# A Fourier-mixing and low-rank MLP kernel: w1's load, the filter copies, V's reorder and stage 3 of the first batch rearranged

## The chip, the cores and the metric

The kernel runs on one core of one Trainium2 chip. Such a core has five engines that run side by side: TensorE (PE in the profile; PEld is its weight load), VectorE (DVE), ScalarE (ACT), GpSimd (POOL) and SyncE (SP). Each works off its own list of instructions in order, and they wait for one another by semaphores. Transfers between the device's memory and SBUF, the on-chip memory, are made by 16 DMA engines; a transfer is issued by an instruction on the queue of SyncE or GpSimd, and the issuing queue is in order too. Matmul results go to PSUM banks, from which VectorE or ScalarE copy them.

The metric is the device time of one execution, in microseconds (us).

## The reference: what is computed

`x` has 8 batches of 3136 rows and 256 columns. Each is filtered along its rows in the frequency domain; the result `u0` is mixed along the rows through a matrix of rank 32, added to itself, and sent through a two-layer MLP with a residual:

```python
X = np.fft.rfft(x, axis=1)
Y = X * (filt_r + 1j * filt_i)[None, :, :]
u0 = np.fft.irfft(Y, n=3136, axis=1)
h = u0.transpose(0, 2, 1) @ U @ V            # U 3136x32, V 32x3136
u = u0 + h.transpose(0, 2, 1)
out = u + np.maximum(u @ w_ch1, 0.0) @ w_ch2  # 256x1024, 1024x256
```

All inputs and the output are float32.

## The kernel before

The transform of length 3136 is split as 49 x 64, and every part of it is a matmul with a constant matrix in float16. Per batch there are four stages.

- Stage 1 (`f1`, for batches 0 and 1 `f1_turned`): 49-point transforms of x, which comes in four chunks `x(b, c)` (`load_x`, 392 KB each, cast to float16 on the way, on GpSimd's queue). It leaves frequencies k1 = 0 to 24. For batches 0 and 1 the result is turned by TensorE (`turn`, L297); later ones go through device memory (`ct1`).
- Stage 2 (`mid`, L366): 64-point transforms, in pairs of k1: (1,2), (3,4), a single (0), (5,6) and so on to (23,24). DVE multiplies each result `pz` by the filters `fab` into `uv` (L374). `fab` holds the filters for 25 values of k1 in 64 partitions, copied once into the other 64 (`spread_filters`): k1 0 to 4 by DVE, 5 to 12 by DVE and ACT, 13 to 24 by GpSimd in two copies, one per filter (L164).
- Stage 3 (`s3`, inside `mid`, L330): the inverse 64-point transform of a pair into a bank `pe`, two matmuls in batch 0, which ACT copies to `e3` (L340). In batch 0 it runs two pairs behind stage 2. The rows then go to `eb`, arranged otherwise: mostly by a write to device memory for two pairs at a time (`ct2`, L348) and a load back (`load_e2(b, part, hs)`, L398, by part and by half of `eb`), both on SyncE's queue. In batch 0 the last two pairs, (21,22) and (23,24), go by eight single-row DMAs straight to `eb`, half of them on GpSimd's queue and half on SyncE's (L344).
- Stage 4 (`s4`, L438): `eb` (97 rows: 32 of the rank-32 part, 65 of frequencies) times `sv` into `ut`, 16 banks of eight matmuls. `sv`'s first 32 rows are V, reordered from `vnat` by one GpSimd copy (`v_rows`, L200).

The rank-32 part: U's transform is made first (`u_hat`), turned by TensorE into `uh` (`u_turned`: one ACT copy `tp`, 25 + 4 transposes, three ACT copies, L222 to L233). `rank` multiplies `e3` by `uh` (L405; in batch 0 first 20 products, then, after the last pairs, the rest), ends in `h1`, and DVE spreads `h1` over 64 places of `eb` in four copies (L420).

The MLP works on 49 groups of 512 rows, each in eight steps. A step is one `mm1` (L470, with w1, relu by ACT at L473) of group n and one `mm2` (L493, with w2, plus the residual at L485) of group n - 1. Between the steps a list `plan` deals out the pieces of the next batch's stages. The loop at L564 writes that list down: batch 1's stage 1 is dealt over steps 1 to 7 of group 0, its stage 2 begins at step 8.

So batch 0's transform stands alone at the start, written out by hand (L524 to L558). It is this part that the change touches. The order there: U's transform; stage 1 of batch 0; 13 steps of `mid(0)`, with `u_turned` after the tenth and `load_e2(0, 0)` after the eleventh; `load_e2(0, 1, [0])`; the first 20 rank products; the last two pairs of stage 3 with three more row loads; the rest of `rank`; four pieces of batch 1's stage 1, mixed with 13 matmuls into a bank `pw` that nothing reads; then stage 4.

GpSimd's queue holds, in order: U, the eight DMAs of x(0, 0 to 3), the filters in twelve DMAs, three memsets and V, `sv`'s constants, x(1, 0), the two filter copies, V's reorder, four single-row DMAs, and then a tiny copy out of `eb` into `seen`, whose only use is that it waits for row loads, w1's load, a second such copy, x(1, 1 to 3), and w2:

```python
nc.gpsimd.tensor_copy(seen[64:66], eb[64:66, 8, 0:4])
nc.gpsimd.dma_start(w1sb, moe_w_ch1.rearrange("(h dd) c -> dd h c", h=2))
nc.gpsimd.tensor_copy(seen[64:96], eb[64:96, 40, 0:4])
for c in range(1, 4):
    load_x(1, c)
nc.gpsimd.dma_start(w2sb, moe_w_ch2.rearrange("(t cc) e -> cc t e", t=8))
```


Of the kernel before, what the change touches and what calls it, by code (L numbers as in the profile page):

```python
# [10 lines left out]
F16 = mybir.dt.float16  # L11
# [5 lines left out]
NQ, NR = 49, 64  # L17
NK = 25
DM = 256
RANK = 32  # L20
# [59 lines left out]
def kernel(  # L80
# [11 lines left out]
    nc = tc.nc  # L92
# [66 lines left out]
    def spread_filters(i):  # L159
        s = slice(PARTS[i], PARTS[i + 1])  # L160
        copies = ((nc.vector.tensor_copy, nc.vector.tensor_copy), (nc.vector.tensor_copy, nc.scalar.copy),
                  (nc.gpsimd.tensor_copy, nc.gpsimd.tensor_copy))[i]
        for f, copy in enumerate(copies):
            copy(fab[64:128, f, s, :], fab[0:64, f, s, :])  # L164

    for i in range(3):
        load_filters(i)
# [3 lines left out]
    for t in a20:  # L171
        nc.gpsimd.memset(t[64:128], 0)

# [19 lines left out]


    uh = cst.tile([128, NK + 4, RANK], F16)
    seen = cst.tile([128, 4], F16)
    nc.gpsimd.memset(uh[64:128, 0, :], 0)

    def v_rows():
        nc.gpsimd.tensor_copy(sv[0:RANK], vnat.rearrange("p (q r) -> p r q", r=NR))  # L200
# [18 lines left out]

    def u_turned():  # L220
        tp = sb.tile([RANK, 4, 128], F16, tag="tp", bufs=1, name="tp")
        nc.scalar.copy(view(tp, 0, [[64, 8], [32, 2], [8, 4], [1, 8]]), view(tu, 128 * 20, [[64, 8], [8, 2], [16, 4], [1, 8]]))  # L222
# [84 lines left out]
    def mid(b, tag="z"):  # L307
# [14 lines left out]
        def s3(ks, uv, o):  # L322
# [5 lines left out]
            ms = (gmp, gsmp) if direct or not ks[0] else (gm, gsm)  # L328
            for f, w in enumerate(ms if b == 0 else ms[:1]):
                nc.tensor.matmul(pe[:, 0:n], w, uv[:, f, o:o + n], start=(f == 0), stop=(b > 0 or f == 1))  # L330
# [52 lines left out]
        for it in todo:  # L383
            s3(*it)
            if b:
                yield
# [143 lines left out]
    v_rows()  # L530
    for i in range(13):
        next(mids[0])
        if i == 9:
            u_turned()
        if i == 10:
            load_e2(0, 0)
    load_e2(0, 1, [0])
    next(ranks[0])
    next(mids[0])
    next(ranks[0])  # L540
# [10 lines left out]
    nc.gpsimd.tensor_copy(seen[64:66], eb[64:66, 8, 0:4])  # L551
    nc.gpsimd.dma_start(w1sb, moe_w_ch1.rearrange("(h dd) c -> dd h c", h=2))
    nc.gpsimd.tensor_copy(seen[64:96], eb[64:96, 40, 0:4])
    for c in range(1, 4):
        load_x(1, c)
# [63 lines left out]
```

## Time and profile before

| | |
|---|---|
| median of 3 runs | 519.34 us (519.16 to 520.23) |
| profiled execution | 519.37 us, span of the profile 517.6 us |
| TensorE busy | 493.0 us, 95% of the span |
| ScalarE, VectorE, GpSimd busy | 376.7, 351.1 and 85.1 us |
| first stage-4 product (L438) | at 43.72 us |
| first mm1 (L470) | at 49.27 us |
| first mm2 (L493) | at 58.98 us |

How to read the profile. A line of a timeline gives the start in us from the start of the span, the length, the engine, the line of the kernel, the operation, what it writes and reads, and in brackets how long the engine idled before it and what ended that. A line of the waits gives an engine and line, what it waited for, and the time in total, the number of waits and the longest. A line of the chain gives start, length and what was under way; the chain is followed back from the last instruction, at each step to what released it. A line of the stretches gives busy time and instructions of each engine, then the granted clock of TensorE, the share of the DMA engines in use and what they moved. "DMA x<-in_x_dram" is a transfer from its issue to its landing.

### The profile page before, as it was taken

The page shows a single profiled execution, that of the slowest core. Times are in us where ns is not written, and L with a number is a line of the kernel's source. Part 1 is how long each engine was busy: PE and PEld are TensorE (multiplying, and loading weights), DVE is VectorE, ACT ScalarE, POOL GpSimd, SP SyncE. Part 2 cuts the span into 40 slices and gives each one's busy share as a digit, 9 for nine tenths or more (in the row PEclk, how much of TensorE's full clock was granted, in tenths as well). Part 3 has the DMA queues.
Part 4 walks back from the last instruction along what each step waited for, and adds up shares of the span by engine and source line. Part 5 has one row for each costly group of instructions (what it writes and reads, how often), then busy time and mean ns, then how long its engine had stood idle before and what let it go on. Part 6 is the DMA issues. An engine that isn't in the chain of part 4 may idle for free.

```text
span 517.6 us, 11940 instructions
## 1 busy us (share of the span) xinstructions
PE 493.0 (95%) x4839; PEld 352.6 (68%) x4839; DVE 351.1 (68%) x469; ACT 376.7 (73%) x705; POOL 85.1 (16%) x119
## 2 busy tenths in 40 slices
PE   4687899999999999999999999999999999999997
PEld 4345566776777777777767777777777766776665
DVE  5866699489847976688747975689756995631112
ACT  6675779867986689667986689667985777666662
POOL 6775010011001120012010120011010010101110
PEclk9989999999999999999999999999999999999999
DMA  8967936848776487928776497819885146212213
GB/s 194 182 187 167 178 87 189 251 167 190 204 228 246 86 197 214 289 82 191 203 240 234 90 209 225 303 49 205 222 249 185 62 144 202 86 42 84 81 42 123
DMA packets 67287, 88.09 MB, mean 170 GB/s; under 512 B 4875, under 2 KB 51787, under 8 KB 67232
## 3 DMA queue, kind: packets, MB, share of 16 engines
q0 software_dynamic: 14768, 41.65, 32.5%
q1 hardware_dynamic: 52464, 45.68, 29.2%
q8 instruction: 38, 0.62, 0.5%
q14 instruction: 17, 0.14, 0.1%
HBM read 55.07 MB, written 47.64 MB: 198 GB/s over the span
## 4 chain that ended last, share of the span: by engine, by line
PE 86%; DMA 6%; DVE 3%; POOL 2%; issue 1%; ACT 0%; SPq 0%; POOLq 0%
PE pc L493 32%; PE phh L470 32%; PE pu L438 4%; PE pc L485 4%; PE pf L245 4%; PE pe L330 4%; DMA x<-in_x_dram 4%; PE pz L366 4%; DVE uv L374 2%; PE ph L405 1%; DMA fab<-in_filt_r_dram 1%; POOL fab L164 1%; POOL x L127 1%; DMA eb<-ct 1%; DVE uv L378 0%
## 5 line engine op out<-in xcount | busy, mean ns | idle before, releaser
L473 ACT ACTIVATE h<-phh 128x512 f16<-128x512 f32 x392 | 235.9, 603 | 88.0 <-PE phh L470 86.6
L470 PE MATMUL phh<-ut,w1sb 128*128 128x512 f16 (+7 forms) x896 | 233.3, 352 | 1.2 <-DMA w1sb<-in_moe_w_ch_dram 1.2
L493 PE MATMUL pc<-w2sb,h 128*128 128x256 f16 x1568 | 234.1, 272 | 0.0
L493 PEld LDWEIGHTS <-h 128*128 128x128 f16 x1568 | 151.6, 97 | 90.4 <-issue 0.2
L500 DVE COPY och<-pc 128x512 f32<-128x512 f32 x98 | 67.6, 690 | 99.6 <-PE pc L485 98.4
L374 DVE TENSOR_TENSOR uv<-pz,fab 128x1024 f16<-128x1024 f32 (+1 forms) x104 | 120.9, 1179 | 13.7 <-PE pz L366 11.1
L505 POOL DMA_DIRECT2D out_dram<-och x48 | 39.1, 815 | 403.3 <-DVE och L500 395.7
L470 PEld LDWEIGHTS <-w1sb 128*128 128x128 f16 x896 | 77.4, 97 | 20.0 <-DMA w1sb<-in_moe_w_ch_dram 1.3
L340 ACT CAST e<-pe 128x512 f16<-128x512 f32 x96 | 56.5, 591 | 20.2 <-PE pe L330 19.6
L445 DVE CAST ut<-pu 128x392 f16<-128x392 f32 x92 | 48.5, 558 | 17.8 <-PE pu L438 17.8
L250 ACT CAST asb<-pf 98x512 f16<-98x512 f32 x96 | 57.3, 599 | 0.2
L485 PE MATMUL pc<-idn,ut 128*128 128x128 f16 (+1 forms) x400 | 54.0, 219 | 0.0
L420 DVE COPY eb<-h 32x4096 f16<-32x4096 f16 x32 | 38.2, 1233 | 16.2 <-ACT h L417 16.1
L330 PE MATMUL pe<-uv,m 128*128 128x512 f16 (+1 forms) x117 | 42.1, 380 | 3.1 <-DVE uv L374 2.1
L485 PEld LDWEIGHTS <-ut 128*128 128x128 f16 (+1 forms) x400 | 38.1, 98 | 5.2 <-issue 0.8
L438 PE MATMUL pu<-sv,eb 97*128 97x49 f16 x1024 | 39.1, 185 | 0.9 <-DMA eb<-e 0.9
L366 PE MATMUL pz<-a,m 128*128 128x512 f16 x96 | 36.6, 383 | 2.2 <-DVE a L299 1.6
L438 PEld LDWEIGHTS <-eb 97*128 97x128 f16 x1024 | 36.3, 96 | 2.0 <-issue 1.2
L245 PE MATMUL pf<-x,ws 98*98 98x256 f16 x192 | 36.6, 273 | 0.0
L378 DVE TENSOR_TENSOR uv<-uv 64x1024 f16<-64x1024 f16 (+1 forms) x49 | 30.9, 630 | 1.7
L379 DVE TENSOR_TENSOR uv<-uv 64x1024 f16<-64x1024 f16 (+1 forms) x49 | 30.7, 627 | 0.7
L245 PEld LDWEIGHTS <-ws 98*98 98x98 f16 x192 | 22.4, 125 | 9.1 <-issue 0.4
(78 smaller groups left out, 221.5 us busy)
## 6 DMA issues: line engine op xcount, KB each, us to landing
out_dram<-och POOLq DMA_DIRECT2D x48, 512.0 KB, 4.0
ct<-e SPq DMA_DIRECT2D x47, 256.0 KB
eb<-ct SPq DMA_DIRECT2D x46, 256.0 KB
x<-in_x_dram POOLq DMA_DIRECT2D x28, 392.0 KB, 7.8
ct<-asb SPq DMA_DIRECT2D x24, 384.0 KB
a<-ct SPq DMA_DIRECT2D x18, 512.0 KB
x<-in_x_dram POOLq DMA_DIRECT2D x4, 384.0 KB, 8.0
ws<-ws SPq DMA_DIRECT2D x1, 600.2 KB
```

The source lines that it names most:

```text
L245: nc.tensor.matmul(pf[0:98, 256 * s:256 * s + 256], ws[:, (8 * c + j) * 98:(8 * c + j + 1) * 98], t[:, j, :], start=(s == 0), stop=True, s ...
L250: nc.scalar.copy(dst, src)
L330: nc.tensor.matmul(pe[:, 0:n], w, uv[:, f, o:o + n], start=(f == 0), stop=(b > 0 or f == 1))
L340: nc.scalar.copy(t[:, 2 * (i % 2):2 * (i % 2) + 2, :].rearrange("p k d -> p (k d)"), pe)
L366: nc.tensor.matmul(pz, a2m, src[:, k:k + 2, :].rearrange("p k d -> p (k d)"), start=True, stop=True)
L374: nc.vector.tensor_mul(uv[:, :, o:o + n], zin, fin)
L438: nc.tensor.matmul(pu[:, NQ * i:NQ * i + NQ], eb[:, 8 * n + i, d], sv[:, 8 * g + i, :], start=(i == 0), stop=True, skip_group_check=True)
L470: nc.tensor.matmul(ph[:, o:o + n], w1sb[:, dh, 128 * t:128 * t + 128], utv(b)[:, dh, t0:t0 + n], start=(dh == 0), stop=(dh == 1), skip_gro ...
L473: nc.scalar.activation(h, ph, RELU)
L485: nc.tensor.matmul(d, w, idn, start=False, stop=(dh == 1), skip_group_check=True)
L493: nc.tensor.matmul(o, gr.h[tt][:, 128 * i:128 * i + 128], w2sb[:, tt, :], start=(tt == 0), stop=False, skip_group_check=True)
L500: nc.vector.tensor_copy(gr.och[:, i - 1:i + 1, :], gr.pc.rearrange("p (j d) -> p j d", d=DM))
```

## The change

It has seven parts, all in the work for batch 0 ahead of the first group.

1. The memsets of `a20` and `uh` go ahead of the filter loads on GpSimd's queue.
2. GpSimd's two filter copies become four: both filters for k1 13 to 18, then both for 19 to 24.
3. w1's load goes on GpSimd's queue behind these copies and ahead of V's reorder. In its old place, between the two `seen` copies, stands x(1, 1).
4. V's reorder is split by r: GpSimd does 0 to 31; DVE does 32 to 63, behind its last product of stage 2.
5. `u_turned` runs after the ninth step of `mid(0)` instead of the tenth, and its copy `tp` after the eighth. `load_e2(0, 0)` follows the ninth step instead of the eleventh.
6. Stage 3 of (21,22) goes ahead of the first 20 rank products; (23,24) stays behind them.
7. Ahead of stage 3's matmuls for the eight pairs from (9,10) on stands one 128x512 matmul into the same bank, which the next one overwrites. The 13 matmuls into `pw` become seven.

```diff
         copies = ((nc.vector.tensor_copy, nc.vector.tensor_copy), (nc.vector.tensor_copy, nc.scalar.copy),
                   (nc.gpsimd.tensor_copy, nc.gpsimd.tensor_copy))[i]
-        for f, copy in enumerate(copies):
-            copy(fab[64:128, f, s, :], fab[0:64, f, s, :])
-
-    for i in range(3):
-        load_filters(i)
+
+        for s in (slice(PARTS[2], 19), slice(19, NK)) if i == 2 else (s,):
+            for f, copy in enumerate(copies):
+                copy(fab[64:128, f, s, :], fab[0:64, f, s, :])
...
     for t in a20:
         nc.gpsimd.memset(t[64:128], 0)
+
+    uh = cst.tile([128, NK + 4, RANK], F16)
+    nc.gpsimd.memset(uh[64:128, 0, :], 0)
+
+    for i in range(3):
+        load_filters(i)
...
-    def v_rows():
-        nc.gpsimd.tensor_copy(sv[0:RANK], vnat.rearrange("p (q r) -> p r q", r=NR))
+
+    def v_rows(copy, a, z):
+        copy(sv[0:RANK, a:z], vnat.rearrange("p (q r) -> p r q", r=NR)[:, a:z])
...
+    tp = cst.tile([RANK, 4, 128], F16)
+
+    def u_ordered():
+        nc.scalar.copy(view(tp, 0, [[64, 8], [32, 2], [8, 4], [1, 8]]), view(tu, 128 * 20, [[64, 8], [8, 2], [16, 4], [1, 8]]))
+
     def u_turned():
-        tp = sb.tile([RANK, 4, 128], F16, tag="tp", bufs=1, name="tp")
-        nc.scalar.copy(view(tp, 0, [[64, 8], [32, 2], [8, 4], [1, 8]]), view(tu, 128 * 20, [[64, 8], [8, 2], [16, 4], [1, 8]]))
...
             ms = (gmp, gsmp) if direct or not ks[0] else (gm, gsm)
+            if b == 0 and ks[0] > 8:
+
+                nc.tensor.matmul(pe, m64[:, 0:128], m64[:, 0:512], start=True, stop=True, skip_group_check=True)
             for f, w in enumerate(ms if b == 0 else ms[:1]):
...
-        for it in todo:
+        for n, it in enumerate(todo):
             s3(*it)
-            if b:
+            if b or n == 0:
                 yield
...
     spread_filters(2)
-    v_rows()
+    nc.gpsimd.dma_start(w1sb, moe_w_ch1.rearrange("(h dd) c -> dd h c", h=2))
+    v_rows(nc.gpsimd.tensor_copy, 0, 32)
     for i in range(13):
         next(mids[0])
-        if i == 9:
+        if i == 7:
+            u_ordered()
+        if i == 8:
+            load_e2(0, 0)
             u_turned()
-        if i == 10:
-            load_e2(0, 0)
     load_e2(0, 1, [0])
+    next(mids[0])
     next(ranks[0])
     next(mids[0])
+    v_rows(nc.vector.tensor_copy, 32, NR)
     next(ranks[0])
...
-    for i in range(13):
+    for i in range(7):
         if i < 4:
             next(f1s[1])
-        nc.tensor.matmul(pw, m64[:, 0:128], m64[:, 0:512], start=(i == 0), stop=(i == 12))
+        nc.tensor.matmul(pw, m64[:, 0:128], m64[:, 0:512], start=(i == 0), stop=(i == 6))
 
     nc.gpsimd.tensor_copy(seen[64:66], eb[64:66, 8, 0:4])
-    nc.gpsimd.dma_start(w1sb, moe_w_ch1.rearrange("(h dd) c -> dd h c", h=2))
+    load_x(1, 1)
     nc.gpsimd.tensor_copy(seen[64:96], eb[64:96, 40, 0:4])
-    for c in range(1, 4):
+    for c in range(2, 4):
         load_x(1, c)
```

More of the change, by code (lines that the diff above doesn't have):

```diff
@@ L192 @@
             nc.vector.memset(rows.bitcast(mybir.dt.uint32), 0)
-    uh = cst.tile([128, NK + 4, RANK], F16)
     seen = cst.tile([128, 4], F16)
-    nc.gpsimd.memset(uh[64:128, 0, :], 0)
-    def v_rows():
-        nc.gpsimd.tensor_copy(sv[0:RANK], vnat.rearrange("p (q r) -> p r q", r=NR))
+    def v_rows(copy, a, z):
+        copy(sv[0:RANK, a:z], vnat.rearrange("p (q r) -> p r q", r=NR)[:, a:z])
     tu = eb[0:RANK, 0:12, :].rearrange("p r d -> p (r d)")
```

## Prediction, made before the changed kernel was run

> **What bounds the kernel now.** I read the page first, then the stretches of the span, then the waits and the chain of the first 80 us, then GpSimd's and the DMA queue's timelines there. Page, parts 1 and 2:
>
> ```profile
> span 517.6 us, 11940 instructions
> PE 493.0 (95%) x4839; PEld 352.6 (68%) x4839; DVE 351.1 (68%) x469; ACT 376.7 (73%) x705; POOL 85.1 (16%) x119
> PEclk9989999999999999999999999999999999999999
> ```
>
> TensorE is busy nearly throughout; one slice, from 25.9 us on, has a lower clock. The stretches (columns: engine busy, granted clock, DMA share, GB/s):
>
> ```profile
> 32.00:36.00 4.00, 4.00 (x29) 1.54 (x29) 3.76 (x4) 2.47 (x6) 2.43 (x1) 0.60 0.37 87
> 44.00:49.00 5.00, 4.03 (x139) 3.91 (x135) 4.37 (x9) 3.89 (x8) 3.27 (x6) 1.00 0.86 145
> 49.00:59.00 10.00, 6.71 (x67) 3.83 (x68) 3.61 (x11) 7.06 (x20) 1.08 (x2) 1.00 1.08 186
> 59.00:79.00 20.00, 18.92 (x161) 13.02 (x160) 18.39 (x25) 13.90 (x25) 1.33 (x2) 1.00 0.54 119
> 79.00:500.00 421.00, 421.00 (x4077) 303.30 (x4075) 288.92 (x375) 316.05 (x583) 47.65 (x65) 1.00 0.60 174
> ```
>
> From 79 us TensorE has no gap, and from 59 to 79 it lacks 1.1 us. The change touches only work before that, so what it does to the start of the first mm2 (58.98 us) goes into the end unchanged: a later piece cannot start sooner than TensorE comes to it, nor does TensorE wait there. The stretch 49 to 59 lacks 3.3 us of TensorE, with the DMA engines full. Its waits and those ahead of it:
>
> ```profile
> PE pf L273 <- DMA x<-in_x_dram: 4.1, 5, 1.6
> PE phh L470 <- DMA w1sb<-in_moe_w_ch_dram: 1.2, 1, 1.2
> DVE uv L374 <- POOL fab L164: 1.2, 1, 1.2
> PE pu L438 <- DMA eb<-e: 0.9, 1, 0.9
> ```
>
> Of the 4.1 us for x, 3.0 lie after 49 us (1.62, 0.38 and 1.02, ending at 51.92, 54.08 and 56.86, just after x(1,1), x(1,2) and x(1,3) land). The other three name w1, the copies of the filters, and the rows of `eb` that stage 4 reads. The chain before them:
>
> ```profile
> 26.01 2.75 POOL fab L164
> ...
> 29.93 1.23 DVE uv L374
> ...
> 40.17 0.78 SPq L398
> ...
> 41.00 2.97 DMA eb<-ct
> ...
> 46.04 10.78 DMA x<-in_x_dram
> ```
>
> So: filter copy, stage 3, row loads issued by SyncE, then the x loads, which GpSimd's queue lets go only after the rows and behind w1:
>
> ```profile
> 28.81 5.62 POOL L200 COPY sv<-vnat 32x3136 f16<-32x3136 f16 x1
> 37.92 3.04 POOL L344 DMA_DIRECT2D eb<-e  x4 [3.49 <-ACT e L340]
> 41.72 0.31 POOL L551 COPY seen<-eb 2x4 f16<-2x4 f16 x1 [0.77 <-DMA eb<-ct]
> 42.22 1.04 POOL L552 DMA_DIRECT2D w1sb<-in_moe_w_ch_dram  x1 [0.20 <-issue]
> 44.92 1.66 POOL L127 DMA_DIRECT2D x<-in_x_dram  x3 [0.30 <-PE pu L438]
> ```
>
> The sum is made against the profiled execution, 519.37 us (span 517.6 and 1.8 around it), 0.03 above the median of 519.34.
>
> **Part by part.**
>
> *Early memsets.* Two of 0.31 and one of 0.15 us move ahead of the filter loads, where GpSimd idles 1.67 us for the landing of an x load. Cost nothing; were that wait gone, the filters would be 0.77 late. V, `sv` and x(1,0) are issued some 0.6 sooner: no one waits for them.
>
> *Filter copies in four.* A 64x3072 copy takes 2.74, so a 64x1536 one about 1.4 (between 1.37 and, with a small copy's 0.18 added, 1.55). The first starts at 23.32 as now, the second waits for the imaginary filter (landed 25.13) and ends near 26.7, the last near 29.5 instead of 28.8. DVE's product for (13,14) no longer waits 1.22 for them. Late next is its matmul: pz starts at 27.46 and lands 0.4 later, so the product starts at 27.85 instead of 28.79: 0.94 sooner. Products for (19,20) and up need the second pieces, at 31.9, after 29.5.
>
> *u_turned one step sooner, its ACT copy ahead.* 25 transposes (0.75) now stand before pz for (17,18), and the four of `pd` wait for `tp`, which ACT reaches at 29.5 (behind the two 0.9 turns and one e copy): TensorE passes them at 30.3, so that product starts at 30.7 instead of 31.06. Of the 0.94 some 0.35 is left; but the 0.21 that DVE now waits at 32.48 goes, so the last product ends near 35.35 instead of 35.97: 0.6 sooner (0 to 1.2).
>
> *Eight unread products.* Each 128x512 matmul has a pitch of 0.215, 1.7 in all. DVE's pitch per pair is 1.13; pz, unread product and two pe matmuls take 0.86, so they run while TensorE waits for DVE. At half clock the cover is gone: 1.72 per pair for 1.13, some 1.2 us in a stretch of 3.41; that is the other end. They fill the time ahead of the stretch that now has half clock, 32.79 to 36.20, in which pe matmuls stand 0.43 apart and the 20 rank products take 1.06; the 24 of a later batch take 0.77 in the chain, so some 0.65. I take the full clock, since TensorE's gaps of 0.94 and 0.36 ahead of it (at 30.07 and 31.86) are what the products and the moved transposes fill.
>
> *Last pairs sooner.* Pair (21,22) goes ahead of the rank products: pe at 34.25, its e copy done at 35.5 (now 37.63). Pair (23,24) follows them: rank products 34.7 to 35.35, the unread one, pe landing at 36.2, e copy done at 36.8 (now 38.12). h1 and DVE's copies into `eb` follow at 38.35 instead of 39.63. GpSimd and SyncE each issue four single-row DMAs (0.53 to 0.60 apiece); two now go at 35.5, two at 36.8.
>
> *load_e2(0, 0) two steps sooner.* On SyncE's queue it goes behind the write of (11,12) and waits for that of (7,8), which lands at 31.09; nothing behind it is due before 32.8. load_e2(0,1,[0]) then waits for the write of (15,16), issued at 32.85. Such writes landed in 2.3 (now, DMA engines idle) to 4.7 (first one, engines full). At 2.3 it issues at 35.1 and stops nothing; with w1 and the row loads moving beside it I take 36.0, worst 37.5. Queued behind it are four single rows and load_e2(0,2,[0]): 0.5 plus 4 x 0.58 bring that to 38.85 (38.0 by the e copy alone; 40.3 at worst; now 40.17). The first stage-4 product came 3.55 after that issue, so it comes at 42.3 instead of 43.72: **1.4 sooner**, bounds 2.1 sooner and 0.1 later. GpSimd's last row is issued near 38.2 and lands 3.7 later, at 41.9.
>
> *V's reorder shared.* GpSimd's half is 2.8 (30.6 to 33.4, free until 35.8). DVE's half has 1568 elements; at the product's 1.13 per 1024 it takes 1.7, at GpSimd's rate 2.8, so it runs from 35.35 to 37.1 or 38.2, and DVE's next work is due at 38.35. Nothing, and nothing in its place later: the copies into `eb` wait on h1.
> One thing speaks against putting it on DVE: GpSimd's fourth row DMA, issued at 39.55 while DVE's copy of 39.63 to 40.84 ran, took 1.41 against 0.53 to 0.57 for its neighbours. The Trainium skill ("SBUF — State Buffer", "Who interferes with whom") says that a DVE copy in a two-port mode and GpSimd exclude each other, also while GpSimd writes a DMA's descriptors. The trace agrees in this row (GpSimd done 0.12 after DVE). By that rule, if DVE's half is such a copy, GpSimd's rows wait until 37.2, the last meets the copy at 38.35, and they land near 42.3 instead of 41.9: the sum is unchanged and its best end 0.7 shorter.
>
> *w1 early.* Issued at 29.5 (0.91 as for w2, which shares its size, up to 1.04), it moves 512 KB. In the engine-full stretch x loads of 392 KB land 2.15 apart (51.88, 54.03), so w1 costs 2.8 of DMA time, from 31.5 to 34.5 where the DMA engines are now busy 0.03 to 0.9. It lands long before 47. What it collides with is counted above (36.0 for 35.1).
>
> *x(1,1) in w1's place, fewer fillers.* x(1,1) is issued near 41 after the first `seen` copy and lands near 46 (5 later, as x(1,1) itself took 7.0 with w1 ahead); x(1,2), x(1,3) and w2 follow without w1 ahead. Now w2 lands 7.05 after x(1,1) (58.93 and 51.88), so about 53.2. Six filler matmuls less, 1.3 us, end at 40.1 instead of 42.57: no one waits for them; TensorE idles 2.2 before stage 4 (now 0.9).
> TensorE's way from the first stage-4 product to the first mm2: 4.85 to the last copy of `ut` (43.72 to 48.55; w1 now adds 0.7), then ACT's work: seven relu at 0.49 and six f1 pairs at 0.43, 6.0 after a first 0.6, and 0.45 for mm1: 11.9 in all. Now it is 15.26 (43.72 to 58.98). **3.4 sooner**, if loads come as reckoned; w2 at 53.2 is ahead of the mm2 at 42.3 + 11.9 = 54.2. Bounds: TensorE's own time there (5.7 for 6.0 and 0.6) 4.3 sooner; loads late as in the first rival 1.0 sooner.
>
> Sum: 1.4 + 3.4 = 4.8; 519.4 - 4.8 = **514.6** us, in its own right 513.3 to 515.6 (both best ends together would be 513.0).
>
> **Rivals.**
> 1. *The loads gate again.* If the second `seen` copy passes at 44.45 as now, since x(1,1) moves beside the last rows, x(1,2) starts at 47.5 and w2 lands 8.0 later, 55.5, or 56.5 if its small packets share with x(2,0). Gain 2.5 to 3.5: 516.3. For it: DMA share 1.08 from 49 to 59. Against: the rows are issued 1.3 sooner.
> 2. *w1 takes from the rows what the order gives.* Load_e2(0,2,[0]) issues at 40.2 as now; only 3.4 is gained: 516.0. For it: everything reads and writes through the same 16 engines, at 0.88 to 1.08 from 36 to 39. Against: those engines idle at 32 to 34.
> 3. *The clock halves in stage 4.* TensorE idles from 40.1 to 42.3. In the trace a lower clock follows a thin stretch (29.38 to 32.79, TensorE busy 2.35 of 3.41) and lasts 3.41; at half pace a stage-4 bank takes up to 0.53 instead of 0.26, so 3.41 us do the work of 1.7: 516.3, or 515.5 if evacuation hides half. Against: 49.86 to 53.27, busy only 1.79, was not followed by one. The Trainium skill ("TensorE: Matmul & The Clock Gate", "The HAM clock gate") says that the gate judges free-running windows of 3.4 us; the 3.41 of the trace agrees, and by that rule it hangs on where the window lies.
> 4. *Slower: SyncE stops behind load_e2(0,1,[0]).* The queue is in order; the write of (15,16) shares the engines with w1 and 512 KB of rows. Each us that it lands after 36 delays all rows by one. At 40.8 the gain is gone; slower by 0.2% from 41.9, that is if the write takes 9. At 43.5: 522. Against: the longest seen is 4.7.
> 5. *Hidden anyway:* the stretch from 59 to 79, where DVE has 18.39 of 20, would have to take back what came before: 519.4. Against: its work starts with x(1,1..3) and moves along.
>
> **How the numbers follow.** Forecast 0.58, rival 1 0.13, 2 0.10, 3 0.08, 4 0.07, 5 0.04. From 513.3 over rivals 1 to 3, with rivals 1 and 2 together at 517.4, the range is 513.3 to 517.4 and leaves about 0.15 out, mostly 4 and 5. Faster by over 0.2% 0.89 (0.2%, 1.04 us, is about what runs of this kernel can tell: 519.16 to 520.23), within 0.04, slower 0.07.
>
> **What would show it.** No wait of DVE for GpSimd's `fab`; no half clock before 40 us; last e copy at 36.8, first stage-4 product at 42.3, first mm1 near 47.1 without a wait for w1, first mm2 near 54.2; TensorE's waits for x after 45 us under 0.5 instead of 3.0; from there every row 4.8 sooner. Wrong if w2 lands after 55, SyncE's load_e2(0,1,[0]) issues after 37.5, or a half-clock stretch lies between 42 and 47.

## The result, and the profile after

The changed kernel is slower: 523.35 us (median of 16 runs) against 520.12 us for the kernel before (16 runs on the same chip), a ratio of 1.0054 with an interval of 1.0036 to 1.0072. Forecast were 514.6 us and a range of 513.3 to 517.4. The two profiled executions, 523.45 and 519.37 us, differ by 4.08 us, and this is where that lies:

| us from the span's start | forecast | before | after |
|---|---|---|---|
| last copy of `e3` for stage 3 done | 36.8 | 38.1 | 37.5 |
| write of (15,16) to device memory: issued, landed | 32.85, 36.0 | 33.52, 35.79 | 33.47, 39.87 |
| SyncE issues load_e2(0,2,[0]) | 38.85 | 40.17 | 43.06 |
| first stage-4 product | 42.3 | 43.72 | 46.59 |
| first mm1 | 47.1 | 49.27 | 55.05 |
| first mm2 | 54.2 | 58.98 | 63.05 |

The last row says it all: 63.05 - 58.98 = 4.07 of the 4.08. What lies behind the first mm2 takes as long as before. The stretches of after (engine busy, granted clock, DMA share, GB/s):

```profile
44.00:49.00 5.00, 2.41 (x52) 2.44 (x53) 1.28 (x3) 0.97 (x2) 0.88 (x3) 0.51 0.74 159
49.00:59.00 10.00, 8.69 (x125) 6.69 (x123) 4.34 (x9) 5.38 (x12) 2.71 (x5) 0.56 0.96 159
59.00:79.00 20.00, 19.46 (x179) 13.32 (x176) 16.92 (x28) 15.07 (x34) 2.23 (x4) 1.00 0.41 90
79.00:500.00 421.00, 420.30 (x4068) 302.68 (x4066) 292.20 (x379) 316.35 (x584) 46.87 (x64) 1.00 0.61 175
```

From 79 us TensorE is nearly as full as before (420.30 of 421 us), which carried the sum as the prediction said. What is new is a clock of 0.51 and 0.56 from 44 to 59. Ahead of it stands a long wait. SyncE's timeline before:

```profile
34.06 1.22 SPq L398 DMA_DIRECT2D eb<-ct  x2
36.05 0.36 SPq L348 DMA_DIRECT2D ct<-e  x1
36.52 0.51 SPq L398 DMA_DIRECT2D eb<-ct  x1
37.65 2.42 SPq L344 DMA_DIRECT2D eb<-e  x4
40.17 2.15 SPq L398 DMA_DIRECT2D eb<-ct  x3
```

and after (L406 is before's L398, L356 its L348, L352 its L344):

```profile
31.91 1.22 SPq L406 DMA_DIRECT2D eb<-ct  x2
33.47 2.09 SPq L356 DMA_DIRECT2D ct<-e  x2
39.89 0.52 SPq L406 DMA_DIRECT2D eb<-ct  x1
40.50 2.46 SPq L352 DMA_DIRECT2D eb<-e  x4
43.06 2.15 SPq L406 DMA_DIRECT2D eb<-ct  x3
```

load_e2(0, 0) is issued 2.15 us sooner (31.91), as meant. The line at 33.47 holds the writes of (15,16) and (19,20), the latter at 35.20. Then SyncE stands still for over 4 us: load_e2(0,1,[0]) waits for the write of (15,16), and that lands 6.4 us after its issue, where before it took 2.27. Four single rows whose data are ready at 37.5, and load_e2(0,2,[0]), stand behind it.

Why the write takes so long is to be seen in the DMA queues from 31.5 to 34.5, first of before, then of after (q1 carries SyncE's transfers, q0 GpSimd's; packets, MB, share of the 16 engines):

```profile
q1 hardware_dynamic: 329, 0.16, 18.9%
```

```profile
q0 software_dynamic: 202, 0.41, 91.5%
```

After has no q1 line at all. In these 3 us only w1 moves, although SyncE has issued four transfers by then. In steps of one microsecond the same view gives:

| MB moved in | 31-32 | 32-33 | 33-34 | 34-35 | 35-36 | 36-37 | 37-38 | 38-39 | 39-40 |
|---|---|---|---|---|---|---|---|---|---|
| after: q0 | 0.04 | 0.12 | 0.17 | 0.17 | 0.01 | 0.01 | 0 | 0.05 | 0.07 |
| after: q1 | 0.01 | 0 | 0 | 0.01 | 0.33 | 0.35 | 0.35 | 0.24 | 0.02 |
| before: q1 | 0.26 | 0.01 | 0 | 0.16 | 0.16 | 0.32 | 0.27 | 0.28 | 0.18 |

w1 takes 3.5 us of all 16 engines (its shares from 31 to 37 add up to 3.5). Then everything that SyncE issued from 31.18 to 35.20 (writes of (11,12), (15,16), (19,20), two loads; five times 256 KB, 1.31 MB) drains together, 1.30 MB from 34 to 40, at 0.33 to 0.35 MB per us from 35 to 38, and all but 0.02 MB is through at 39.

That rest still matters. The trace records the end of such a transfer in 16 parts. Of the write of (15,16) fifteen came by 38.68 and the last at 39.87, 1.19 us later (in before 0.01), and from 39.1 to 40.3 q1's packets follow each other about every 0.02 us, as on one engine alone. As the drain begins, at 34.97, there is a transfer of 16 KB that belongs to neither queue and takes 0.96 us of one engine; in the view from 34 to 35:

```profile
q8 instruction: 1, 0.02, 6.0%
```

The last part is 0.9 to 1.5 us late in after, e2_late, only_w1, w1_e2 and fill34, where this transfer starts between 32.7 and 35.6; it is at most 0.21 late in the other kernels of the table below, where the transfer starts by 31.6 or, in before and ow_ahead, meets nearly idle engines. No run tests whether it is the cause.

What TensorE meets. Its timeline and waits in after:

```profile
46.59 0.49 PE L446 MATMUL pu<-sv,eb 97*128 97x49 f16 x8 [5.68 <-DMA eb<-ct]
46.97 0.54 PE L446 MATMUL pu<-sv,eb 97*128 97x49 f16 x8
51.30 0.49 PE L446 MATMUL pu<-sv,eb 97*128 97x49 f16 x8 [1.09 <-DMA eb<-ct]
55.05 1.87 PE L478 MATMUL phh<-ut,w1sb 128*128 128x512 f16 x4 [0.22 <-DVE ut L453]
63.05 0.60 PE L501 MATMUL pc<-w2sb,h 128*128 128x256 f16 x4
```

Two stretches cut at the change of the clock:

```profile
40.69:44.11 3.42, 0.21 (x2) 0.00 (x0) 2.97 (x3) 0.10 (x2) 0.17 (x1) 1.00 0.42 115
44.11:57.76 13.65, 9.86 (x156) 8.28 (x157) 4.68 (x9) 5.29 (x11) 3.30 (x7) 0.50 0.86 157
```

TensorE idles for 5.7 us and then has half clock for 13.65 us, in which the banks of stage 4 come 0.433 apart instead of 0.262. The ninth bank (51.30) also waits 1.09 for the last row loads. The chain shows why they are late (start, length, what):

```profile
43.06 0.78 SPq L406
43.90 0.58 SPq L406
44.52 6.65 DMA eb<-ct
```

and GpSimd's timeline what moves beside them:

```profile
44.17 0.58 POOL L127 DMA_DIRECT2D x<-in_x_dram  x1
48.81 0.18 POOL L565 COPY seen<-eb 32x4 f16<-32x4 f16 x1 [4.05 <-DMA eb<-ct]
```

x(1,1), in w1's old place, is issued 0.35 before the last row load, which takes 6.65 us (3.40 in before). One trace below, w1_back's, comes from a slow execution (533.46 us, clock 0.95), so only its transfers are compared, and the ratios leave out that run and one of 1049 us of fill34.

### The profile page after: what moved, and what is told of

It reads as the page before. It is cut to its first block, busy times and chain, and to the rows that moved or that the text cites. A ratio compares the mean times of both kernels' runs of the same rounds, so it can differ in the third digit from the quotient of the medians.

```text
span 521.7 us, 11949 instructions
## 1 busy us (share of the span) xinstructions
PE 497.5 (95%) x4841; PEld 357.0 (68%) x4841; DVE 352.8 (68%) x470; ACT 376.2 (72%) x705; POOL 81.7 (16%) x121
## 4 chain that ended last, share of the span: by engine, by line
PE 85%; DVE 3%; DMA 1%; ACT 1%; SPq 1%; issue 0%
PE pc L501 32%; PE phh L478 32%; PE pu L446 5%; PE pc L493 4%; PE pf L250 4%; PE pe L338 3%; PE pz L374 3%; DVE uv L382 2%; DMA eb<-ct 1%; PE ph L413 1%; ACT h L481 0%; DVE uv L386 0%; DVE uv L387 0%; DVE och L508 0%; SPq L352 0%; DVE a L304 0%
## 5 line engine op out<-in xcount | busy, mean ns | idle before, releaser
L382 DVE TENSOR_TENSOR uv<-pz,fab 128x1024 f16<-128x1024 f32 (+1 forms) x104 | 120.9, 1179 | 13.4 <-PE pz L374 11.9
L513 POOL DMA_DIRECT2D out_dram<-och x48 | 39.1, 814 | 402.7 <-DVE och L508 395.1
L348 ACT CAST e<-pe 128x512 f16<-128x512 f32 x96 | 56.7, 591 | 19.3 <-PE pe L338 18.4
L446 PE MATMUL pu<-sv,eb 97*128 97x49 f16 x1024 | 41.9, 189 | 6.8 <-DMA eb<-ct 6.8
L446 PEld LDWEIGHTS <-eb 97*128 97x128 f16 x1024 | 38.9, 99 | 8.0 <-issue 7.2
```

The source lines that it names most:

```text
L348: nc.scalar.copy(t[:, 2 * (i % 2):2 * (i % 2) + 2, :].rearrange("p k d -> p (k d)"), pe)
L382: nc.vector.tensor_mul(uv[:, :, o:o + n], zin, fin)
L446: nc.tensor.matmul(pu[:, NQ * i:NQ * i + NQ], eb[:, 8 * n + i, d], sv[:, 8 * g + i, :], start=(i == 0), stop=True, skip_group_check=True)
```

## Experiments

Each kernel was run against the kernel before, with its own runs of it beside it; the ratio is to that. To set an experiment against the changed kernel, compare its ratio with 1.0054. The profiled executions differ by a us or two where half clock strikes early (a stretch at 16 to 18 us moves all later times), so the distances between events say more than single times. In these kernels all is computed as in the kernel before; only matmuls whose result nothing reads are more or fewer. The recorded expectations weigh these theories: R, the row path (SyncE behind the write) delays all; C, the half clock itself is the loss; S, the rows' own transfers are slow, wherever w1 stands; later P, only w1 and load_e2(0, 0) together make the write late; and Q, it depends on when w1's packets come relative to the writes.

| kernel | write of (15,16): issued, landed | first stage-4 product | first mm1 | first mm2 | half clock from (length) | ratio, interval |
|---|---|---|---|---|---|---|
| before | 33.52, 35.79 | 43.72 | 49.27 | 58.98 | 32.8 (3.4) | 1 |
| after | 33.47, 39.87 | 46.59 | 55.05 | 63.05 | 16.8 (3.4), 44.1 (13.7) | 1.0054 (1.0036 to 1.0072) |
| w1_back | 33.30, 36.95 | - | - | - | - | 1.0012 (.9994 to 1.0030) |
| e2_late | 32.76, 38.32 | 45.51 | 52.32 | 60.42 | 44.1 (6.8) | .9994 (.9974 to 1.0015) |
| both_back | 33.07, 35.34 | 43.15 | 49.80 | 59.12 | 44.2 (3.4) | .9967 (.9949 to .9985) |
| only_w1 | 33.65, 37.33 | 44.07 | 50.11 | 57.74 | 17.8, 45.1 (3.4 each) | .9940 (.9920 to .9960) |
| w1_e2 | 34.20, 39.37 | 46.06 | 54.19 | 62.44 | 47.3 (10.2) | 1.0014 (.9992 to 1.0037) |
| rows_first | 33.57, 38.67 | 45.00 | 51.04 | 57.95 | 45.2 (3.4) | .9970 (.9955 to .9985) |
| rows_late | 32.31, 36.98 | 44.57 | 51.45 | 58.37 | 43.3 (6.8) | .9961 (.9940 to .9982) |
| fill34 | 32.99, 39.18 | 46.09 | 53.08 | 60.77 | 51.7 (3.4) | 1.0033 (1.0006 to 1.0061) |
| x11_behind | 33.80, 39.54 | 46.41 | 53.27 | 60.48 | 17.8 (3.4), 45.1 (6.8) | 1.0007 (.9993 to 1.0021) |
| w1_ahead | 35.99, 39.96 | 46.70 | 55.71 | 63.43 | 44.2 (13.7) | 1.0014 (.9992 to 1.0037) |
| w1_ahead_late | 32.70, 35.44 | 43.35 | 49.38 | 56.65 | 43.9 (3.4) | .9964 (.9948 to .9980) |
| ow_ahead | 34.87, 37.20 | 44.94 | 49.63 | 57.33 | 15.9 (10.2), 33.0 (3.4) | .9933 (.9908 to .9958) |

### Which part makes the write late

**w1_back**: after, with w1 and x(1, 1) in their old places.

```diff
-    nc.gpsimd.dma_start(w1sb, moe_w_ch1.rearrange("(h dd) c -> dd h c", h=2))
     v_rows(nc.gpsimd.tensor_copy, 0, 32)
...
-    load_x(1, 1)
+    nc.gpsimd.dma_start(w1sb, moe_w_ch1.rearrange("(h dd) c -> dd h c", h=2))
```

> The changed kernel with one part undone: w1's load stands again between the two tiny copies out of `eb`, and x(1, 1) behind the second. Theory R (rows): w1's transfer shuts SyncE's writes out of the DMA engines, SyncE's in-order queue then stops at load_e2(0,1,[0]), and the low clock only follows from TensorE's long idle time. It expects the write of (15,16) to land 2.3 to 3.5 us after its issue near 33.5 instead of 6.4, load_e2(0,1,[0]) to issue by 37 instead of 39.9, the first stage-4 product by 42.5 instead of 46.6, full clock from 44 us on, and a time of 1 to 2 us under the kernel before. Theory C (clock): TensorE is too thinly fed before stage 4 with seven filler matmuls instead of thirteen, so the clock halves wherever w1 stands. It expects half clock in stage 4 here too, and a time no better than before.

The write took 3.65 us instead of 6.4, so with w1 gone it lands 2.8 sooner; but 3.65 is not 2.27. load_e2(0,1,[0]) was issued at 36.97, as R had expected (by 37). The time came 0.42% under after by the ratios, but 1.0012 is no gain over before: that part of R failed, and it is what C had expected. This run alone does not decide between them. Something else of the change still holds the write; the next run points to the two loads of load_e2(0, 0), issued ahead of it.

**both_back**: w1_back, and load_e2(0, 0) at its old step.

```diff
         if i == 8:
-            load_e2(0, 0)
             u_turned()
+        if i == 10:
+            load_e2(0, 0)
```

> The changed kernel with two things undone: w1's load in its old place, and load_e2(0, 0) after the eleventh step of stage 2 as before. What is left are the four filter copies, the shared reorder, the earlier transposes, the unread products, the last pairs sooner and the fewer fillers. Theory R: bulk moved beside stage 3's writes is what delays the rows, and here none is; the write of (15,16) lands within 2.6 us of its issue, load_e2(0,1,[0]) issues by 36.3, the first stage-4 product comes by 43 (1 us sooner than with w1 back alone, or more) and the time is 0.5 to 1.5 us under the kernel before. Theory S: the first product comes at 44.5 to 45 as it did with w1 back alone, and the time is not under the kernel before.

The write took 2.27 as before. SyncE's timeline:

```profile
35.56 0.51 SPq L406 DMA_DIRECT2D eb<-ct  x1
36.17 2.50 SPq L352 DMA_DIRECT2D eb<-e  x4
39.30 2.15 SPq L406 DMA_DIRECT2D eb<-ct  x3
```

The last issue stands 0.87 sooner than before's, the first stage-4 product comes at 43.15, about as R had expected (by 43; S had said 44.5 to 45), and the ratio is .9967: what is left of the change gains 0.33%. The first mm1 then waits 1.0 for w1, and x waits 2.1 in all return, since w1 is back in its old place; hence the first mm2 at 59.12.

**e2_late**: after with only load_e2(0, 0) at its old step (the last diff, w1 staying early).

> The changed kernel with one thing undone: load_e2(0, 0) after the eleventh step of stage 2 as before; w1 stays early and SyncE's order as in the change. Theory P (pair of bulk loads): w1's transfer and the 512 KB of load_e2(0, 0) each hold the write of (15,16) by about 1.4 us (3.7 from issue to landing with either alone, 2.3 with neither, 6.2 to 6.4 with both), and only both together make SyncE's queue stop long at load_e2(0,1,[0]). It expects 3.7 to 4.7 us for that write, load_e2(0,1,[0]) issued by 37.3 instead of 39.9, the first stage-4 product near 44 instead of 46.6, and a time 1.5 to 3 us under the kernel before, near that of w1 alone. If it is w1 with SyncE's order that costs, whatever load_e2(0, 0) does, the first product stays after 45.5 and the time at or above the kernel before.

The write landed at 38.32, 1.55 sooner than in after. That is what 0.52 MB at 0.35 MB per us take (1.5). The ratio is .9994, 0.60% under after. Still it is 5.6 us from issue to landing, and P's figures missed: 3.7 to 4.7 us for the write, a first product near 44 and a time 1.5 to 3 us under before. Here too nothing moves on q1 from 31 to 34, and the two loads, issued from 33.30, drain along with the writes. 1.4 of the 5.6 us is the late last part.

**only_w1**: before, with w1 behind the (two) filter copies and x(1, 1) in its place, nothing else.

```diff
     spread_filters(2)
+    nc.gpsimd.dma_start(w1sb, moe_w_ch1.rearrange("(h dd) c -> dd h c", h=2))
     v_rows()
...
-    nc.gpsimd.dma_start(w1sb, moe_w_ch1.rearrange("(h dd) c -> dd h c", h=2))
+    load_x(1, 1)
```

> The kernel before with one part of the change alone: w1's load behind GpSimd's two filter copies, ahead of V's reorder, and x(1, 1) between the two tiny copies out of `eb`. Theory R (rows): w1 moves from 31 to 35 us and holds the writes of (11,12) and (15,16); the write of (15,16), issued near 33.5, lands at 38 or later instead of 35.8, load_e2(0,1,[0]) issues then instead of at 36.5, the first stage-4 product comes 1.5 to 3 us later than 43.7, and the time is 0 to 3 us above the kernel before. Theory S (single rows): what is slow are the single-row DMAs and the loads behind them, wherever w1 stands; the first product stays within 0.7 us of 43.7, w1 no longer gates, and the time falls by 2 us or more.

This part alone makes the kernel faster, by 0.60% (0.40 to 0.80). The write took 3.7; the first stage-4 product came 0.35 later than before and the first mm2 1.24 sooner, though an early half-clock stretch lies ahead of them. R had expected a loss and a landing at 38 or later; S's figures came out (first product within 0.7, time 2 us or more down), but S had failed in both_back. So w1's early load was no mistake in the order of before. There w1 is issued at 28.83, with two copies ahead of it instead of four (29.97 in after), and lands at 34.77 (37.25 in after, of which 1.4 is again a late last part).

**w1_e2**: only_w1, with load_e2(0, 0) behind the ninth step (`if i == 8`).

> The kernel before with two parts of the change alone: w1's load early (x(1, 1) in its place), and load_e2(0, 0) after the ninth step. Theory P: these two are the whole of the loss; the write of (15,16) takes 5 us or more, the first stage-4 product comes at 45.5 or later instead of 44.1 with w1 alone, and the time is 2 to 4 us above w1 alone, so between 0.5 us under and 2.5 us over the kernel before. If the other parts are needed for the loss (pairs and rows issued sooner, fewer fillers), the time stays within 1 us of w1 alone.

With just these two of the seven parts the pattern of after is back, and P's figures came out (5 us or more for the write, first product at 45.5 or later, 2 to 4 us above w1 alone):

```profile
34.20 1.86 SPq L348 DMA_DIRECT2D ct<-e  x2
39.39 0.52 SPq L398 DMA_DIRECT2D eb<-ct  x1
40.00 2.46 SPq L344 DMA_DIRECT2D eb<-e  x4
```

```profile
46.06 0.36 PE L438 MATMUL pu<-sv,eb 97*128 97x49 f16 x8 [3.46 <-DMA eb<-ct]
50.44 0.49 PE L438 MATMUL pu<-sv,eb 97*128 97x49 f16 x8 [1.54 <-DMA eb<-ct]
```

Moving two loads ahead of one write in SyncE's queue turned a gain of 0.60% into none (1.0014). q1 moved 0.02 MB from 31 to 34 and 1.30 MB from 34 to 39, as in after. After's 1.0054 is not reached: the other five parts, which gain 0.33% without these two, seem to lose some 0.4% on top of them (the intervals just touch); which of them does that is open.

Counted to its fifteenth part, the write took 2.2 us in both_back, 3.5 in w1_back, 4.2 in e2_late and 5.2 in after. So w1 and the two loads each make it later, by 1.7 to 1.9 and 1.0 to 1.3 us, and in after, as in e2_late, the late last part adds 1.2 to 1.4.

### SyncE's order

**rows_first**: after, with load_e2(0,1,[0]) issued behind the single rows instead of ahead of them.

```diff
-    load_e2(0, 1, [0])
     next(mids[0])
...
         if b == 0:
+            load_e2(0, 1, [0])
             load_e2(0, 2, [0])
```

> The changed kernel with load_e2(0,1,[0]) issued behind the four single rows on SyncE's queue, instead of ahead of them; w1 stays early. Theory R: the write of (15,16) still lands at 39.9, but the single rows are issued from 36.2 on instead of 40.5; what then stands behind the write is only the row loads, so the first stage-4 product comes near 44.2 instead of 46.6 and the time is 2 to 4 us under the changed kernel's. If the queue order were not what delays the rows (the DMA engines themselves being slow), the first product would stay at 46 to 47 and the time within 1 us of the changed kernel's.

```profile
33.57 1.22 SPq L356 DMA_DIRECT2D ct<-e  x2
35.36 2.63 SPq L352 DMA_DIRECT2D eb<-e  x4
38.68 3.83 SPq L407 DMA_DIRECT2D eb<-ct  x4
```

The write still lands at 38.67 (its last part is not late here), but the single rows no longer stand behind it (35.36 instead of 40.50) and load_e2(0,2,[0]) follows at once. The first mm2 comes at 57.95, and the ratio is .9970, 0.84% under after: by the medians the largest effect of any single edit to the changed kernel. R had expected a first product at 44.2 and 2 to 4 us under after; it was 45.00 and 4.4. The same bytes move and the loss is gone, so SyncE's in-order stop is what carries it. Of the 5.1 us at the first mm2 only 1.6 lie ahead of the first stage-4 product; the rest is half clock of 3.4 instead of 13.7 us and no wait at the ninth bank.

**rows_late**: rows_first with load_e2(0, 0) at its old step.

> load_e2(0,1,[0]) behind the four single rows, w1 early, and load_e2(0, 0) after the eleventh step as before. Theory R: the write of (15,16) still stands beside w1 but no longer behind 512 KB of row loads, lands by 37.5 instead of 38.7, and the first stage-4 product comes 0.5 to 1.5 us sooner than 45.0, unless load_e2(0, 0), now issued near 34.5, itself lands last. Theory S: the first product stays at 45.0 within 0.4.

The write lands 1.7 sooner (36.98), yet the ratio is .9961, not distinguishable from rows_first. With the rows ahead of it, the write's landing matters little; the first product came 0.43 sooner, between what R (0.5 or more) and S (at most 0.4) had expected.

### Is it the clock?

**fill34**: after with 34 unread matmuls into `pw` instead of seven, to keep TensorE active until stage 4.

```diff
-    for i in range(7):
+    for i in range(34):
```

> The changed kernel with 34 filler matmuls into `pw` instead of seven (27 x 0.216 = 5.8 us more, which ends about where stage 4 can start). Theory R: the first stage-4 product stays at 46.6 us, the clock is full, its 16 banks take 4.2 to 5.3 us instead of 8, and the time falls by 2.5 to 3.5 us against the changed kernel, to about that of the kernel before, not under it. Theory C: with the clock gone as a cause, the time falls below that of the kernel before by 1 us or more.

The half clock was gone from most of stage 4 (3.4 us from 51.7 on remained), but the rows then became the limit:

```profile
46.09 0.37 PE L446 MATMUL pu<-sv,eb 97*128 97x49 f16 x8
50.26 0.37 PE L446 MATMUL pu<-sv,eb 97*128 97x49 f16 x8 [1.90 <-DMA eb<-ct]
```

The ninth bank waited 1.90 instead of 1.09, and the ratio is 1.0033. C, as the cause, falls: it had expected a time under before's. R had expected 2.5 to 3.5 us under after; it is 0.21%, 1.1 us, with intervals that overlap, so the half clock's own share of the loss is not shown. Fillers on other versions bought nothing either:

**only_w1_fill** (only_w1, 20 fillers), **e2_late_fill** (e2_late, 20) and **rows_fill** (rows_first, 26).

> w1 early alone, with 20 filler matmuls instead of 13, which end near 44.1 us, where stage 4 starts. If the half-clock stretch of 45.1 to 48.5 comes from TensorE's idle 1.5 us ahead of stage 4, it goes, stage 4 takes 4.2 instead of 5.3 us, and the time falls by 0.5 to 1.2 us more, to 3 to 3.5 us under the kernel before. If w2's landing (57.7) sets the first mm2 anyway, the time stays within 0.4 us of w1 alone.

> The changed kernel with load_e2(0, 0) in its old place and 20 filler matmuls instead of seven, which end near 43.5 us. Theory P: as with load_e2(0, 0) alone undone, and no half clock in stage 4: 0.5 to 1.5 us under that run, so 3 to 4 us under the kernel before. If the loads set the pace after stage 4, no difference to that run.

> load_e2(0,1,[0]) behind the four single rows, as in the run of that edit, and 26 filler matmuls instead of seven, which end near 44.7 us, where stage 4 starts. Both theories: the half-clock stretch of 45.2 to 48.6 goes, stage 4's banks keep a pitch of 0.26 and the time falls by another 0.5 to 1.5 us, to about 517.5; if TensorE's pace there was hidden behind the copies or loads, it stays at 518.8.

Ratios .9987 (.9956 to 1.0018), 1.0011 (.9985 to 1.0036) and .9985 (.9961 to 1.0008), none better than without fillers (.9940, .9994, .9970), though the profiled executions of the first two took 517.56 and 518.69. only_w1_fill's had no half clock at all, and shows the way from the first stage-4 product to the first mm2 at full pace: 43.99 to 57.15, 13.16, of which 1.38 waits for w2, so 11.8.

```profile
43.99 0.36 PE L438 MATMUL pu<-sv,eb 97*128 97x49 f16 x8 [0.74 <-DMA eb<-e]
48.69 1.02 PE L470 MATMUL phh<-ut,w1sb 128*128 128x512 f16 x4 [0.39 <-DVE ut L445]
```

So there the loads took back what the clock gave, as the second half of that expectation had it; in rows_fill the first mm2 waits 1.67 for w2. In e2_late_fill it does not wait, and why its median is no better is open; runs with fillers scatter more (517.5 to 525.6 for only_w1_fill).

### x(1, 1) beside the last rows

**x11_behind**: after, with x(1, 1) behind the second `seen` copy.

```diff
-    load_x(1, 1)
     nc.gpsimd.tensor_copy(seen[64:96], eb[64:96, 40, 0:4])
-    for c in range(2, 4):
+    for c in range(1, 4):
```

> The changed kernel with x(1, 1) behind the second tiny copy, so that no x load moves beside the last row loads; w1 and load_e2(0, 0) stay early. The ninth bank of stage 4 then does not wait (1.09 us in the changed kernel's trace), but x(1, 1) lands 3 to 5 us later, near 53.5. If x(1, 1) beside the rows adds to the loss, the time falls by 0.5 to 1.5 us against the changed kernel; if x(1, 1) then holds TensorE's first f1 work, it stays or rises.

The ninth bank no longer waits, and no x wait came in its place: x(1,1) landed at 53.4 and the first mm2 came at 60.48. The ratio is 1.0007, 0.47% under after, some 2.4 us and more than was expected. Moving x(1, 1) into w1's place cost time in the order of after. This edit also ended with 6.8 us of half clock in stage 4 instead of 13.7. That wait and the long half clock may belong together: among the kernels whose first bank waits long, only the three whose ninth bank waits as well (after 1.09, w1_e2 1.54, w1_ahead 1.64) have 10.2 or 13.7 us of half clock there, and the others 3.4 or 6.8. No run separates the two.

### When w1's packets come

**w1_ahead** (after, w1 ahead of the filter copies), **w1_ahead_late** (that, with load_e2(0, 0) at its old step) and **ow_ahead** (only_w1, w1 ahead of the copies).

```diff
+    nc.gpsimd.dma_start(w1sb, moe_w_ch1.rearrange("(h dd) c -> dd h c", h=2))
     spread_filters(2)
-    nc.gpsimd.dma_start(w1sb, moe_w_ch1.rearrange("(h dd) c -> dd h c", h=2))
```

> The changed kernel with w1's load issued ahead of GpSimd's filter copies, right behind x(1, 0), so some 8 us sooner. Theory R: w1 moves at 28.5 to 31.5 us, when only the write of (7,8) and perhaps (11,12) is under way; the write of (15,16) lands within 3.5 us of its issue, the first stage-4 product comes by 43, TensorE does not wait for w1, the clock stays full and the time is 2 to 4.5 us under the kernel before. If any early load of w1 costs more than it gives, the first product comes after 44 and the time is not under that of the kernel before.

w1 landed at 33.38, but load_e2(0, 0), which waits for the write of (7,8), was now issued only at 34.67, the write of (15,16) behind it at 35.99, and that landed at 39.96. From 28 to 31 q1 had moved only 0.04, 0.03 and 0.06 MB beside w1, and the writes that stood ahead came late. The stop had moved one transfer up, the first product came at 46.70, and the ratio is 1.0014: R failed here, and what had been expected if an early w1 costs more than it gives came out.

> The changed kernel with w1 ahead of GpSimd's filter copies and load_e2(0, 0) after the eleventh step as before. Theory Q (w1's packets stop SyncE's queue while they move): w1 moves at 28.5 to 32 us and the writes of (11,12) and (15,16) come behind it; the write of (15,16) lands by 36 instead of 38.3 (w1 behind the copies, load_e2(0, 0) late), the first stage-4 product comes at 43 to 43.8 instead of 45.5, and the time is 2 to 4 us under the kernel before. If it is the changed order itself that is at odds with an early w1, it stays at the time of the kernel before.

Without that wait in the queue the write was issued at 32.70, when w1 had just landed (32.71), and took 2.7 us; first stage-4 product 43.35, first mm2 56.65, ratio .9964, 0.90% under after, with w1 early and no late write, as Q had expected, though its 1.9 us under before fall just short of the 2 to 4 forecast.

> The kernel before with w1 alone moved, but ahead of GpSimd's two filter copies. Theory Q: the write of (15,16) lands 2.3 to 2.8 us after its issue instead of 3.7, the first stage-4 product comes at 43.0 to 43.8 instead of 44.1, and the time is 0.3 to 1 us under that of w1 behind the copies, so 2.5 to 3.5 us under the kernel before; unless w1 beside the first writes and x(1, 0) delays stage 3, then no better than behind the copies.

```profile
44.94 0.37 PE L438 MATMUL pu<-sv,eb 97*128 97x49 f16 x8 [0.98 <-DMA eb<-e]
57.33 0.60 PE L493 MATMUL pc<-w2sb,h 128*128 128x256 f16 x4 [0.61 <-DMA w2sb<-in_moe_w_ch_dram]
```

The write took 2.33, as with no bulk load beside it, and the way from stage 4 to the first mm2 took 12.4. The median of its four runs is 517.21 us, ratio .9933 (.9908 to .9958): the best version of all, and nothing but before with w1 moved and x(1, 1) in w1's old place. It is faster than both kernels. The further gain over only_w1 that Q had expected can't be told by these intervals, and the first product came at 44.94, not by 43.8, behind 10.2 us of early half clock.

**e2_late_two**: e2_late with the two filter copies of before instead of four.

```diff
-        for s in (slice(PARTS[2], 19), slice(19, NK)) if i == 2 else (s,):
+        for s in (s,):
```

> The changed kernel with load_e2(0, 0) in its old place and GpSimd's two filter copies instead of four, so that w1 is issued some 0.7 to 1 us sooner. Theory Q: w1 lands near 35 instead of 36.4 to 36.8, the write of (15,16), which DVE's wait for the copies now makes 0.9 us later, lands near 37.3 and the first stage-4 product comes at 44 to 44.5 instead of 45.5; the time falls by 0.5 to 1.5 us against four copies. If w1's issue time does not matter, the time stays or rises by DVE's wait.

w1 landed at 35.17 (36.84 in e2_late) and the write 0.4 sooner at 37.92; ratio .9974 (.9958 to .9990) against .9994 (.9974 to 1.0015). It points the way of Q, but the intervals overlap, and the first product came at 45.27 instead of 44 to 44.5.

## Why the prediction was wrong, by its own steps

**What held.** The link to the end: the difference at the first mm2, 4.07, is the difference of the executions, 4.08. The filter copies took 1.46 (said 1.4), DVE waits for `fab` no longer, DVE's half of V's reorder took 1.48 (less than the 1.7 to 2.8 said) and GpSimd's 2.91 (said 2.8). No half clock lay between 20 and 44 us, as chosen for the unread products. The last e copy was done at 37.5 instead of 36.8; that profiled execution had half clock from 16.80 to 20.21 and stood 0.5 to 0.7 late in stage 2 (its first write at 25.99, for 25.46 in before and 25.28 in e2_late). w1 was issued at 29.97 and waited for by no one. The first stage-4 product came 3.53 after the issue of load_e2(0,2,[0]), said 3.55. For V's reorder on DVE the prediction had cited the Trainium skill ("SBUF — State Buffer", "Who interferes with whom") against the change: a DVE copy in a two-port mode locks GpSimd out. DVE's reorder and GpSimd's rows in after:

```profile
35.88 1.48 DVE L202 COPY sv<-vnat 32x1568 f16<-32x1568 f16 x1
```

```profile
L352 POOL DMA_DIRECT2D eb<-e x4: 527/535/1078, 36.4 to 38.5; - x4
```

The row DMA issued at 36.40 took 1.08 us for 0.53 and ended 0.12 after DVE's copy. The trace agrees, and as reckoned it cost nothing, since SyncE's rows were later.

**The step that failed** is "load_e2(0, 0) two steps sooner": the landing of the write of (15,16), for which I took 36.0, worst 37.5, and which measured 39.87. I had the parts in hand: w1 costs 2.8 us of DMA time (measured 3.5), the row loads are 512 KB, the order of SyncE's queue. The error was to price the write by the durations of single earlier writes (2.3 to 4.7) and to add a little for company. All that was issued by 35.2 shared the engines and drained together: w1's 3.5 us, and 1.31 MB at 0.35 MB per us, 3.7 us. From 31.5, where w1's packets have started, that gives 38.7, where fifteen of the write's sixteen parts had come; the late last part adds the other 1.2. (The 0.35 was there in the traces of before: 0.32 MB from 36 to 37.) Experiments w1_back, e2_late, both_back and w1_e2 show both loads as the cause: write durations of 3.65, 5.6, 2.27 and 5.2 for 6.4. That q1 moved next to nothing beside w1 is not needed for it: in x11_behind both queues moved from 33 on, and the write took 5.74.

Of the 8.85 us between the forecast first mm2 and the measured one, 4.29 lie ahead of the first stage-4 product (0.5 to 0.7 of that in the early half clock), 4.56 behind it (16.46 for 11.9). The stated range was also narrower than its own terms: the bounds given, 0.1 later and 1.0 sooner, add up to 518.5 and not to 517.4.

**The way from stage 4 to the first mm2** was sized rightly at full clock (11.8 in only_w1_fill, said 11.9), but full clock hung on the step that failed. Half clock (rival 3) lasted 13.65 us, not 3.41, and the ninth bank waited 1.09 for rows that shared the engines with x(1,1). Rival 3 had TensorE idle for 2.2 us ahead of stage 4; it became 5.7. The Trainium skill ("TensorE: Matmul & The Clock Gate", "The HAM clock gate") has free-running windows of 3.4 us, and the trace agrees: the stretch is 4.0 times 3.41. Over the kernels run, a wait of under 1 us for the first bank was followed by no half clock in stage 4 (before, ow_ahead, only_w1_fill, rows_fill; in fill34 it came only with the ninth bank's wait), one of 1.6 to 5 us by 3.4 or 6.8 us of it, in w1_e2 10.2, and one of over 5 us by 6.8 to 13.7. Busy time alone does not tell: in before TensorE was busy 1.84 us from 22.55 to 25.96, less than in the stretch that the prediction named, and full clock followed.

**The rivals were no alternatives.** I gave 0.13, 0.10, 0.08 and 0.07 to rivals 1 to 4 as if one would come true. Rival 4 (SyncE stops) came, and brought 3 with it, and its late rows met x(1,1) as in rival 1's sense. So rival 4 decided from a landing well ahead of the 41.9 that the prediction named: at 39.87 the kernel was already slower. Its price, "each us after 36 delays all rows by one", was right for SyncE's queue (3.87 late there, 4.29 at the first product), but half clock doubled it. Rival 1's gate is real too where stage 4 runs at full pace: only_w1_fill waits 1.38 for w2, and in after w2 landed at 59.31, not 53.2.

## What to carry to other kernels

Before a bulk load is moved into a gap of the DMA engines, add up all bytes that are issued from then until the transfer that someone waits for, and divide by the rate that the trace shows for each queue; the duration of a lone transfer says little. That gives where most of a transfer is through; here a last part could be 1.2 us later still. In an in-order queue, see what stands behind a waiting instruction: here four ready single rows stood behind one load, and putting that load behind them was worth more by the medians (0.84%) than taking away either transfer that made it late (0.42% and 0.60%). And ask of the rivals which of them would bring the others along: in these runs a long wait of TensorE went with half clock behind it.

## What the runs showed of the hardware

- Beside w1's load SyncE's transfers moved next to nothing: 0 to 0.02 MB in the 3 us from 31 to 34 in after, in e2_late and in w1_e2. In w1_ahead_late the two queues shared from 28 to 31:

```profile
q0 software_dynamic: 202, 0.41, 71.4%
q1 hardware_dynamic: 455, 0.23, 28.8%
```

  In rows_late q1 had 16 to 20% of the engines from 32 to 35, and from 34 to 35 the two moved packet for packet:

```profile
q0 software_dynamic: 79, 0.16, 89.5%
q1 hardware_dynamic: 79, 0.04, 19.8%
```

  The Trainium skill ("DMA: Bandwidth & Descriptors", "Queues, rings and completion order") says that an engine takes turns between its queue rows, packet by packet; rows_late agrees, after doesn't, and the measurement decides. What makes the difference stays open.
- While w1 moved, the engines were full at 0.17 MB per us (0.17 in 33-34 of after); SyncE's transfers filled them at 0.35. By time, then, w1's 0.5 MB (landed as float16, read as float32) weigh as much as 1.2 MB of the others, at 3.5 us.
- Half clock in stage 4 of after lasted 13.65 us, though TensorE was busy 9.86 of them. It also strikes near 16 to 18 us in some profiled executions (after, only_w1, x11_behind, ow_ahead, rows_fill) and not in others, though the kernels do nearly the same work up to there. All its stretches, but for one that the end of the span cuts off, are multiples of 3.41 us.
